# A planned order for attention and two expert layers: new priorities, and instruction packets in the planner's model of the DMA rings

## The chip, the cores and the metric

The kernel runs on one core of a Trainium2 chip. Its time is the device time in microseconds of one execution; where one number stands for a kernel it is the median of its timed runs. Five engines work beside each other and meet only at semaphores: TensorE (PE; its weight loads are shown apart as PEld), VectorE (DVE), ScalarE (ACT), GpSimd (POOL) and SyncE (SP), which issues the transfers here. A transfer is spread over 16 DMA engines.

## What is computed

Three stages follow one another. The first is a local attention beside an attention on a sequence that is reduced by four; the second a feed-forward layer with a rational activation; the third a feed-forward layer with h·tanh(softplus(h)).

```python
# q, k, v: [2, 8, 576, 64] float32
q_d, k_d, v_d = (mean of 4 neighbours along the sequence)            # 144 rows
out_up    = repeat(softmax(q_d k_d^T / 8) v_d, 4)
out_local = softmax(q k^T / 8 where |i - j| < 4, else -1e9) v
x = (out_up + out_local), as 1152 tokens x 512
h = x @ w_in1                                                        # 512 x 2048
P = a0 + a1 h + a2 h^2 + a3 h^3;  Q = 1 + |b0| |h| + |b1| h^2
x = (P / (Q + 1e-6)) @ w_out1                                        # 2048 x 512
h = x @ w_in2
out = (h * tanh(softplus(h))) @ w_out2
```

The weights arrive as 64-bit floats (read as int64 words) and are converted on the chip.

## The kernel before

**Attention.** There are 18 units: one batch, one pair of heads and four windows of 64 query rows each, two of them mixed (the last window of all four head pairs of a batch). A unit is a chain: SyncE loads q (L648) and four pieces of v windows (L665); TensorE flips q (L552, 128x128) and, after a copy by ScalarE or VectorE, makes the scores (L712 to L728); VectorE takes the maxima (L743) and subtracts them (L752), ScalarE takes exponentials (L759, L767), VectorE and GpSimd normalise (L772 to L786); TensorE transposes the result (L797, L802) and multiplies it with v (L827, L837); the sum goes to x as a high and a low part (L857 and behind). Each of the eight pairs of heads needs its keys loaded and flipped once (L560, L564, L552 with 96 columns) and its v reduced (L614). There are two buffers for v windows and three for q, so a load of windows waits for the value products of the unit two before it.

**Weights.** They come in grains of 1 MB (L994 for the first matrix of a layer, L999 for the second), into two raw buffers. ScalarE converts in two steps (L1011, L1018), VectorE joins them (L1025; for most grains of the last layer also L1031), and a high and a low part are split off (L1037, L1042).

**Products.** Each product of float32 is made of three passes (high by high, low by high, high by low). L1155 are those of the second stage's first matrix, L1288 and L1290 those of the second matrices, L1469 and L1525 those of the third stage's first matrix. They follow the attention in chunks of tokens, so the products of the first chunk (256 tokens) start while later chunks are still in attention. VectorE and ScalarE evaluate the activation between the two matrices (for the first group by a division on VectorE, L1184 to L1255).

**What sets the order.** Nothing is ordered by hand. While the program is built, `Plan.run` simulates the engines with a cost per task, and each engine that is free takes the ready task of lowest priority number. Instructions are emitted in the order in which this simulation starts them, and on the chip each engine keeps that order and waits where it must. The priorities come from constants and two tables: `PROL` and `PSTEP` space the attention units of the first chunk, `LEAD` says how far the later ones run ahead of the products that need them, `UOFF` shifts each of the 18 units; `LOFF`, `KOFF`, `VOFF` and `VROFF` shift the loads of q, k, v windows and v; `LLEAD` and `CLEAD` put the loads and the conversion of weights ahead of their first use, `OLAG` shifts the second matrices, `GOFF` the first twelve grains. Where TensorE has nothing to do in the simulation and the recent share of it is under `FILL`, a dummy product of zeros (L533) is put in. The model of transfers has one queue: a transfer starts after the one before it has moved, at most eight are under way (`QUEUED`).

The functions that the diff touches:

Of the kernel before, what the change touches and what calls it, by code (L numbers as in the profile page):

```python
# [25 lines left out]

SECOND = 1.8
COLD, FILL_ALL = 3.4, 20
WINDOW, FILL, FILL_END = 3.4, 0.9, 450.0
SHOW = (2.4, 30.0)  # L30
LEAD, CLEAD, LLEAD, OLAG = 38, 14, 40, 18
PROL, PSTEP, VOFF, VROFF, LOFF, KOFF = -45, 2.5, 2, -1, 7, 9
GROUPS = ([6, 6, 4], [4, 4, 4, 4])
KCUT, MIX = 4, (1, 4)
MKP = -45
# [3 lines left out]
NRAW, NWT, NRING, NRING2 = 2, 2, 3, (2, 1)  # L39
LAT = {"pe": 0.2, "act": 0.16, "dve": 0.15, "pool": 0.15, "sp": 1.1}  # L40
QUEUED = 8
UOFF = [-3.0, 0.0, 0.0, 3.0, 4.5, 3.0, 3.0, -1.5, 6.0, 0.0, 0.0, -4.5, -4.5, 4.5, 6.0, 4.5, -1.5, -1.5]
GOFF = [0.0, 0.0, 0.0, 0.0, -4.0, -4.0, -10.0, -6.0, 2.0, -4.0, 10.0, 12.0]
HP = 15


# [34 lines left out]
class Plan:  # L81
# [33 lines left out]
    def run(self, names):  # L115
# [3 lines left out]
        landed, moved = [0.0] * QUEUED, 0.0  # L119
# [76 lines left out]
        while True:  # L196
            for e in names:
# [3 lines left out]
                while ready[e]:  # L201
# [18 lines left out]
                    end = until[e] = begin + t.engs[e] * (2 if e == "pe" and now < COLD else 1)  # L220
                    there = end + LAT[e]
                    if t.dma:
                        end = begin
                        for issue, move in t.dma:
                            end = max(end, landed[-QUEUED]) + issue
                            moved = max(moved, end + 0.3) + move
                            landed.append(moved + LAT["sp"])
                        until[e], there = end, landed[-1]
                    n += 1
# [13 lines left out]
                if e == "pe" and until[e] <= now:  # L243
                    got = fill()
                    if got:
                        b, dur = got
                        end = until[e] = now + dur * (2 if now < COLD else 1)
# [27 lines left out]
def kernel(  # L275
# [26 lines left out]
    add = plan.add  # L302
# [184 lines left out]
    t_id = add({"pool": 1.1}, lambda: make_identity(nc, ident), -1000)  # L487
    t_m = add({"dve": 0.1}, lambda: nc.vector.memset(band, 0.0), -1900)
    t_cd = add({"dve": 0.6}, zeros, -1000)
    add({"dve": 0.4}, lambda: None, -880)  # L490
    t_bn = add({"pool": 0.5}, bands, -900, after=[t_m])
    def mask_set(lo, hi, ws):
        for w in ws:
            masks(*w)
# [2 lines left out]
    t_mk = [  # L497
        add({"dve": cost}, lambda x=x: mask_set(*x), pr, after=[t_bn])
        for cost, pr, x in (
            (0.4, -890, (0, 4, ((0, 0, 1), (0, 1, 1), (0, 2, 1), (0, 3, 1)))), (0.25, MKP, (3, 7, ((1, 4, 4),))),  # L500
            (0.25, MKP, (7, 11, ((2, 8, 4),))),
        )
    ]
    t_bias = add({"pool": 0.1}, biases, -20)
# [129 lines left out]
    def unit(u, slots, start):  # L634
        bb, kind, wins, prio, nw, n = u.bb, u.kind, u.wins, u.prio, NW, 32 * NW
        pairs = sorted({p for p, _ in wins})
        mixed = len(pairs) > 1
# [68 lines left out]
        def pe_b():  # L706
# [24 lines left out]
                        )  # L731

        tb = add(
            {"pe": 1.6 if mixed else 0.86}, pe_b, prio,
            after=tq + [kv_done[p] for p in pairs] + [t_i16, t_mk[kind]],
            take=[sc, tm, s, pd],
            use=[qT] + mix, chain="pb",
# [157 lines left out]
    first = [(0, 256), (256, 256), (512, 256), (768, 384)]  # L895
# [689 lines left out]
```

## Time and profile before

| | |
|---|---|
| timed runs | 477.99, 479.17, 482.95 us; median 479.17 |
| profiled execution | 481.31 us, its span 479.5 us |
| mean granted TensorE clock | 0.993 |
| busy, share of the span | PE 98%, PEld 89%, DVE 79%, ACT 70%, POOL 12% |
| instructions | 9855; 4081 matmuls |
| transfers | 47.17 MB, 97 GB/s over the span |

The span runs from the first to the last instruction of the profiled execution. Busy time is shown for each engine; matmuls are pipelined, so that their rows overlap. A row of a timeline has its start in the span, its duration, engine, source line, operation, what it writes and reads, and in square brackets the idle time of that engine before it, with the engine that ended it. In a stretch, the column PEclk is the TensorE clock that was granted, as a share of full speed: 1.00 and 0.50 are its two levels, 2.4 and 1.2 GHz.

### The profile page before, as it was taken

How to read it: one execution, taken by the hardware profiler on the slowest of the kernel's cores; microseconds unless marked ns; L12 is line 12 of the kernel's file. 1: busy time of each engine (PE TensorE's matmuls, PEld its weight loads, DVE VectorE, ACT ScalarE, POOL GpSimd, SP SyncE). 2: the span in 40 equal slices, each digit the busy share in tenths (PEclk: the TensorE clock that was granted, in tenths of full speed). 3: DMA queues.
4: the chain of work that ended last, by engine and by line, in shares of the span. 5: the costliest groups of instructions: out<-in, count | busy, mean ns of one | idle time of the engine just before them, and what ended most of it. 6: DMA issues, size and time to landing. Idle time of an engine off the chain costs nothing.

```text
span 479.5 us, 9855 instructions
## 1 busy us (share of the span) xinstructions
PE 467.6 (98%) x4081; PEld 428.5 (89%) x4081; DVE 376.8 (79%) x566; ACT 337.6 (70%) x529; POOL 58.7 (12%) x80
## 2 busy tenths in 40 slices
PE   8999898999999999999999999999999999999996
PEld 4667797889999999999999998898989898989885
DVE  6688789899899978997999989988596669524342
ACT  5778698885988799998878797578667446422320
POOL 2654345653000000000000000000000000000000
PEclk9999799999999999999999999999999999999999
DMA  8967976611422402333022022134314220000103
GB/s 180 234 172 176 263 184 182 153 42 36 168 89 90 143 34 87 106 130 117 0 89 89 1 89 87 45 115 143 137 21 156 87 89 0 1 0 2 66 1 131
DMA packets 45757, 47.17 MB, mean 98 GB/s; under 512 B 30352, under 2 KB 31120, under 8 KB 45712
## 3 DMA queue, kind: packets, MB, share of 16 engines
q1 hardware_dynamic: 45712, 46.54, 33.4%
q8 instruction: 32, 0.52, 0.5%
q14 instruction: 13, 0.11, 0.1%
HBM read 44.17 MB, written 2.36 MB: 97 GB/s over the span
## 4 chain that ended last, share of the span: by engine, by line
PE 74%; DVE 12%; DMA 8%; ACT 3%; issue 1%; SPq 1%; ACTq 0%
PE psum L1290 19%; PE psum L1155 18%; PE psum L1288 15%; PE psum L1469 11%; PE psum L1525 5%; DMA att<-in_q_dram 3%; DMA raw<-in_moe_w_in_dram 3%; PE psum L837 1%; DMA att<-in_v_dram 1%; PE psum L827 1%; DVE wt L1025 1%; PE psum L552 1%; DVE xl L1311 1%; DVE wrk L1329 1%; PE psum L728 1%
## 5 line engine op out<-in xcount | busy, mean ns | idle before, releaser
L1155 PE MATMUL psum<-xh,wi 128*128 128x384 f32 (+1 forms) x336 | 84.7, 323 | 0.2 <-DVE wrk L1184 0.2
L1288 PE MATMUL psum<-gg,wo 128*128 128x384 f32 (+1 forms) x480 | 76.2, 313 | 0.0
L1288 PEld LDWEIGHTS psum<-gg,wo 128*128 128x128 f32 x480 | 72.8, 189 | 0.5 <-issue 0.2
L1155 PEld LDWEIGHTS psum<-xh,wi 128*128 128x128 f32 x336 | 60.2, 193 | 1.5 <-issue 0.9
L1155 PE MATMUL psum<-xl,wi 128*128 128x384 f32 (+1 forms) x168 | 53.1, 316 | 0.0
L1290 PE MATMUL psum<-wo,gg 128*128 128x512 f32 x216 | 51.7, 391 | 0.0
L1290 PE MATMUL psum<-wo,late_g 128*128 128x512 f32 x216 | 51.3, 391 | 0.0
L1290 PEld LDWEIGHTS psum<-wo,late_g 128*128 128x128 f32 x216 | 40.4, 188 | 8.0
L1290 PEld LDWEIGHTS psum<-wo,gg 128*128 128x128 f32 x216 | 40.4, 188 | 8.0
L1025 DVE SCALAR_TENSOR_TENSOR wt<-wt,raw 128x1024 int32<-128x1024 int32 x32 | 40.4, 1266 | 7.5 <-ACT wt L1011 6.5
L1011 ACT ACTIVATE wt<-raw 128x1024 f32<-128x1024 f32 x32 | 36.4, 1137 | 8.7 <-DVE wo L1042 4.8
L1018 ACT ACTIVATE raw<-raw 128x1024 int32<-128x1024 uint16 x32 | 36.8, 1149 | 4.7 <-DMA raw<-in_moe_w_out_dram 3.4
L1525 PE MATMUL psum<-xh,wi 128*128 128x384 f32 x128 | 34.5, 335 | 0.0
L1155 PEld LDWEIGHTS psum<-xl,wi 128*128 128x128 f32 x168 | 32.5, 193 | 0.0
L1401 DVE TENSOR_TENSOR part<-psum,part 128x512 f32<-128x512 f32 x27 | 17.8, 687 | 13.6 <-PE psum L1290 13.6
L1155 PE MATMUL psum<-xh,late_r 128*128 128x384 f32 x96 | 25.5, 334 | 0.0
L1175 ACT ACTIVATE wrk<-psum 128x768 f32<-128x768 f32 (+1 forms) x27 | 19.9, 735 | 6.6 <-PE psum L1155 6.0
L1037 ACT ACTIVATE wo<-wt 128x1024 fp32r<-128x1024 f32 x11 | 11.7, 1061 | 17.7 <-DVE wt L1031 7.7
L1042 DVE TENSOR_TENSOR wo<-wt,wo 128x1024 fp32r<-128x1024 f32 x14 | 17.1, 1218 | 8.7 <-ACT wo L1037 8.7
L1525 PEld LDWEIGHTS psum<-xh,wi 128*128 128x128 f32 x128 | 23.3, 188 | 0.2
L1099 ACT ACT_TABLE_LOAD x17 | 21.8, 1283 | 0.3
L1525 PE MATMUL psum<-xl,wi 128*128 128x384 f32 x64 | 21.4, 335 | 0.0
(164 smaller groups left out, 1038.5 us busy)
## 6 DMA issues: line engine op xcount, KB each, us to landing
raw<-in_moe_w_in_dram SPq DMA_DIRECT2D x16, 1024.0 KB, 5.4
raw<-in_moe_w_out_dram SPq DMA_DIRECT2D x16, 1024.0 KB, 4.9
att<-in_v_dram SPq DMA_DIRECT2D x72, 48.0 KB, 4.0
out_dram<-part SPq DMA_DIRECT2D x9, 256.0 KB, 2.0
att<-in_q_dram SPq DMA_DIRECT2D x16, 128.0 KB, 3.9
att<-in_k_dram SPq DMA_DIRECT2D x6, 288.0 KB, 3.8
att<-in_v_dram SPq DMA_DIRECT2D x6, 288.0 KB
wrk<-in_k_dram SPq DMA_DIRECT2D x2, 288.0 KB, 6.2
```

Of the source, the lines that this page charges most:

```text
L1011: nc.scalar.activation(out=t.v, in_=words(r)[:, :, 1].bitcast(F32), func=AF.Prelu if fold else AF.Identity, scale=2.0 ** -112, **({"alpha" ...
L1018: nc.scalar.activation(out=words(r)[:, :, 0], in_=r.v.bitcast(U16).rearrange("p (n four) -> p n four", four=4)[:, :, 1], func=AF.Copy, sca ...
L1025: nc.vector.scalar_tensor_tensor(out=ti, in0=ti, scalar=3, in1=words(r)[:, :, 0], op0=ALU.logical_shift_left, op1=ALU.bitwise_or)
L1042: ENG[e].tensor_tensor(out=w.v[:, 1], in0=s.v, in1=w.v[:, 0].bitcast(F32), op=ALU.subtract)
L1099: nc.scalar.preload_act_table_set(name)
L1155: nc.tensor.matmul(st.h.v[:, i, :T], w.v[:, ww, ks], xx[:, kk, c0:c0 + T], start=(nn == 0 and (st.big or i == 0)), stop=(nn == 3 * KD - 1 ...
L1175: nc.scalar.activation(out=vw(st.a), in_=H(), func=AF.Square)
L1288: nc.tensor.matmul(A(d)[:, :T], w.v[:, ww, lo + d * 128:lo + (d + 1) * 128], vw(gg)[:, i, :], start=start, stop=stop)
L1290: nc.tensor.matmul(A(d), vw(gg)[:, i, sl], w.v[:, ww, lo:lo + DM], start=start, stop=stop)
L1401: nc.vector.tensor_tensor(out=pv, in0=acc.v[:, j], in1=pv, op=ALU.add)
L1469: nc.tensor.matmul(dst.v[:, :TW], wv.v[:, ww, at:at + 128], x(h, kk), start=bool(take) and nn == 0, stop=nn == 5, skip_group_check=not take,)
L1525: nc.tensor.matmul(h.v[:, i, :TW], w.v[:, ww, at:at + 128], xx[:, kk, c0:c0 + TW], start=nn == 0, stop=nn == 3 * KD - 1)
```

## The change

It alters the costs and priorities that the planner works with, and one rule in its model. Line numbers of the changed program are higher by one from the model of transfers on.

```diff
-WINDOW, FILL, FILL_END = 3.4, 0.9, 450.0
-SHOW = (2.4, 30.0)
-LEAD, CLEAD, LLEAD, OLAG = 38, 14, 40, 18
-PROL, PSTEP, VOFF, VROFF, LOFF, KOFF = -45, 2.5, 2, -1, 7, 9
+WINDOW, FILL, FILL_END = 3.4, 0.7, 450.0
+LEAD, CLEAD, LLEAD, OLAG = 38, 20, 30, 26
+PROL, PSTEP, VOFF, VROFF, LOFF, KOFF = -45, 3.0, 2, 2, 5, 9
...
-UOFF = [-3.0, 0.0, 0.0, 3.0, 4.5, 3.0, 3.0, -1.5, 6.0, 0.0, 0.0, -4.5, -4.5, 4.5, 6.0, 4.5, -1.5, -1.5]
-GOFF = [0.0, 0.0, 0.0, 0.0, -4.0, -4.0, -10.0, -6.0, 2.0, -4.0, 10.0, 12.0]
+FETCH = (0.8, 7.0)
+SHOW = (2.4, 30.0)
+UOFF = [1.5, 0.0, 1.5, 9.0, 13.5, 13.5, 6.0, 18.0, 13.5, 9.0, 3.0, -6.0, -7.5, -3.0, 9.0, 12.0, -7.5, -7.5]
+GOFF = [0.0, 2.0, 8.0, 4.0, 0.0, -4.0, -4.0, -22.0, 18.0, 0.0, -6.0, 24.0]
...
                         for issue, move in t.dma:
                             end = max(end, landed[-QUEUED]) + issue
-                            moved = max(moved, end + 0.3) + move
+                            first = max(moved, end + 0.3)
+                            moved = first + move + FETCH[0] * (int((first + move) / FETCH[1]) - int(first / FETCH[1]))
                             landed.append(moved + LAT["sp"])
...
-    add({"dve": 0.4}, lambda: None, -880)
-    t_bn = add({"pool": 0.5}, bands, -900, after=[t_m])
+    t_bn = add({"pool": 1.0}, bands, -900, after=[t_m])
...
-            (0.4, -890, (0, 4, ((0, 0, 1), (0, 1, 1), (0, 2, 1), (0, 3, 1)))), (0.25, MKP, (3, 7, ((1, 4, 4),))),
-            (0.25, MKP, (7, 11, ((2, 8, 4),))),
+            (0.8, -890, (0, 4, ((0, 0, 1), (0, 1, 1), (0, 2, 1), (0, 3, 1)))), (0.5, MKP, (3, 7, ((1, 4, 4),))),
+            (0.5, MKP, (7, 11, ((2, 8, 4),))),
...
-            {"pe": 1.6 if mixed else 0.86}, pe_b, prio,
+            {"pe": 1.52 if mixed else 0.78}, pe_b, prio,
```

`FETCH` adds 0.8 us to a modelled transfer each time it passes a multiple of 7 us: the time in which instruction packets take the rings. The costs of the mask's set-up rise, an empty task that stood in for some of it goes, and the scores' cost falls by 0.08. The rest is numbers.

In the built programs the work is the same, but for two things: 66 dummies instead of 61, and one copy of 128x768 sums that ScalarE made (L1368) is now made by VectorE (L512). All else is moved. Three places show how.

On SyncE, around the first load of weights: L665 are pieces of v windows, L648 loads of q, raw_74 is the first raw buffer of weights; in brackets stand the semaphores waited for. Before:

```order
L665 DMA att<-in_v_dram 48x4x64 [waits DMAHW2_49]
L648 DMA att<-in_q_dram 128x4x64 [waits DMAHW3_49,PE_49]
L994 DMA raw_74<-in_moe_w_in_dram 128x4x256 [waits DMAHW4_49]
L648 DMA att<-in_q_dram 128x4x64 [waits DMAHW5_49,PE_49]
L665 DMA att<-in_v_dram 48x4x64 [waits DMAHW6_49,PE_49]
L665 DMA att<-in_v_dram 48x4x64 [waits DMAHW7_49,PE_49]
L665 DMA att<-in_v_dram 48x4x64 [waits DMAHW0_49,PE_49]
```

In the changed program, one line higher each:

```order
L666 DMA att<-in_v_dram 48x4x64 [waits DMAHW4_49,PE_49]
L666 DMA att<-in_v_dram 48x4x64 [waits DMAHW5_49,PE_49]
L666 DMA att<-in_v_dram 48x4x64 [waits DMAHW6_49,PE_49]
L666 DMA att<-in_v_dram 48x4x64 [waits DMAHW7_49]
L649 DMA att<-in_q_dram 128x4x64 [waits DMAHW0_49]
L995 DMA raw_74<-in_moe_w_in_dram 128x4x256 [waits DMAHW1_49]
```

The four pieces that wait for TensorE stood behind the first weights and stand ahead of them now.

On TensorE, from the tenth unit's scores (the first two rows) on: L827 and L837 are value products, L552 flips of k (96 columns) and q (128), L797 and L802 transposes of the softmax, L1288 products of the second matrix. Before, the tenth unit's transposes are the last two rows:

```order
L720 MATMUL psum<-att 32x48 x16
L728 MATMUL psum<-att 32x144 x4
L827 MATMUL psum<-att 64x64 x4
L837 MATMUL psum<-att 64x32 x16
L797 MATMUL psum<-ident,att 112x128 x2
L802 MATMUL psum<-ident,att 72x128 x2
L1288 MATMUL psum<-gg,wo_81 128x256 x12
L552 MATMUL psum<-ident,att 128x96 x6
L552 MATMUL psum<-ident,att 128x128 x2
L797 MATMUL psum<-ident,att 112x128 x2
L802 MATMUL psum<-ident,att 72x128 x2
```

In the changed program the tenth unit's scores are again the first two rows, its transposes the last two:

```order
L721 MATMUL psum<-att 32x48 x16
L729 MATMUL psum<-att 32x144 x4
L798 MATMUL psum<-ident,att 112x128 x2
L803 MATMUL psum<-ident,att 72x128 x2
L828 MATMUL psum<-att 64x64 x4
L838 MATMUL psum<-att 64x32 x16
...
L721 MATMUL psum<-att 32x48 x16
L729 MATMUL psum<-att 32x144 x4
L798 MATMUL psum<-ident,att 112x128 x2
L803 MATMUL psum<-ident,att 72x128 x2
```

Before, the unit ahead had its values and its transposes there, and twelve products and eight flips besides; now one set of transposes, one of values and the scores of the next unit are all that is between.

On VectorE, the same unit's softmax: L743, L744 are the maxima, L752 the subtraction, L772 to L776 the sums and their reciprocals; L1213 and L1218 belong to the activation, L857 to another unit's sum. Before:

```order
L743 TENSOR_REDUCE att<-psum 128x4
L744 TENSOR_REDUCE att<-psum 128x1
L1213 SCALAR_TENSOR_TENSOR wrk<-wrk 128x512
L857 TENSOR_TENSOR att<-psum,att 128x256
L752 TENSOR_TENSOR att<-psum,att 128x4x48
L1218 SCALAR_TENSOR_TENSOR wrk<-wrk,cf 128x512
L772 TENSOR_REDUCE att<-att 128x4
L773 TENSOR_SCALAR att<-att 128x5
L776 RECIPROCAL att<-att 128x5
```

In the changed program:

```order
L744 TENSOR_REDUCE att<-psum 128x4
L745 TENSOR_REDUCE att<-psum 128x1
L753 TENSOR_TENSOR att<-psum,att 128x4x48
L1026 SCALAR_TENSOR_TENSOR wt_76<-wt_76,raw_74 128x1024
L773 TENSOR_REDUCE att<-att 128x4
L774 TENSOR_SCALAR att<-att 128x5
L777 RECIPROCAL att<-att 128x5
L858 TENSOR_TENSOR att<-psum,att 128x256
```

Two steps of the activation and the other unit's sum no longer stand between the tenth unit's maxima and its reciprocals; a join of weights (L1026) does.

## Rows read from the trace of the kernel before

**Rows 1.** The page's first part: busy time, share of the span and instructions.

```profile
PE 467.6 (98%) x4081; PEld 428.5 (89%) x4081; DVE 376.8 (79%) x566; ACT 337.6 (70%) x529; POOL 58.7 (12%) x80
```

**Rows 2.** Stretches: from:to, length, busy (instructions) per engine, PEclk, DMA share, GB/s.

```profile
50.00:60.00 10.00, 8.50 (x114) 7.41 (x113) 7.09 (x15) 5.58 (x14) 4.03 (x5) 0.66 1.00 271
60.00:120.00 60.00, 57.42 (x1134) 51.41 (x1133) 55.45 (x115) 49.26 (x115) 29.80 (x34) 1.00 0.48 119
120.00:310.00 190.00, 189.14 (x1116) 187.34 (x1114) 174.42 (x196) 162.37 (x190) 0.75 (x1) 1.00 0.25 84
```

**Rows 3.** Timeline of SyncE's queue: start, time (us), engine, line, operation.

```profile
15.37 0.51 SPq L994 DMA_DIRECT2D raw<-in_moe_w_in_dram  x1
16.84 0.61 SPq L648 DMA_DIRECT2D att<-in_q_dram  x1
17.55 2.04 SPq L665 DMA_DIRECT2D att<-in_v_dram  x4
...
36.75 3.33 SPq L665 DMA_DIRECT2D att<-in_v_dram  x4
```

**Rows 4.** Timeline of TensorE, 13.6 to 16.5 us.

```profile
13.70 0.38 PE L797 MATMUL psum<-ident,att 128*112 128x128 f32 x2
...
14.13 0.57 PE L533 MATMUL psum<-blank 128*128 128x480 bf16 x2
14.63 0.26 PE L712 MATMUL psum<-mask,eye 64*32 64x192 bf16 x4
...
15.41 0.45 PE L827 MATMUL psum<-att 72*64 72x64 f32 x8
...
16.39 0.30 PE L552 MATMUL psum<-ident,wrk 96*128 96x96 f32 x1
```

**Rows 5.** Timeline of ScalarE: the first weight conversion's two steps.

```profile
22.91 1.14 ACT L1011 ACTIVATE wt<-raw 128x1024 f32<-128x1024 f32 x1
...
24.55 1.15 ACT L1018 ACTIVATE raw<-raw 128x1024 int32<-128x1024 uint16 x1
```

**Rows 6.** Timeline of TensorE; in brackets idle time before and what ended it.

```profile
30.77 0.46 PE L1155 MATMUL psum<-xh,wi 128*128 128x256 f32 x1
...
39.94 0.41 PE L552 MATMUL psum<-ident,att 128*128 128x128 f32 x2 [0.51 <-DMA att<-in_q_dram]
...
52.51 1.03 PE L837 MATMUL psum<-att 48*64 48x32 f32 x30 [1.50 <-DMA att<-in_v_dram]
...
76.57 0.69 PE L552 MATMUL psum<-ident,att 96*128 96x96 f32 x5 [1.13 <-ACT att L593]
77.99 0.40 PE L797 MATMUL psum<-ident,att 128*112 128x128 f32 x2 [0.72 <-POOL att L786]
```

**Rows 7.** The stretch behind the wait at 52.51, columns as before.

```profile
52.60:59.40 6.80, 6.80 (x95) 6.02 (x96) 4.18 (x9) 3.59 (x9) 1.62 (x3) 0.50 1.03 250
```

**Rows 8.** Landing times of one line's loads: L994 first, then L648.

```profile
DMA to landing us min/median/max: 5.2/5.4/7.9
...
DMA to landing us min/median/max: 2.1/3.9/6.6
```

**Rows 9.** Timeline of all engines, 71.7 to 78.1 us: TensorE and VectorE rows.

```profile
71.79 0.41 PE L728 MATMUL psum<-att 64*32 64x144 f32 x8
...
72.88 0.35 DVE L743 TENSOR_REDUCE att<-psum 128x4 f32<-128x192 f32 x1
...
73.36 0.74 DVE L1213 SCALAR_TENSOR_TENSOR wrk<-wrk 128x512 f32<-128x512 f32 x1
...
73.52 1.68 PE L1288 MATMUL psum<-gg,wo 128*128 128x256 f32 x12
...
74.62 0.73 DVE L1218 SCALAR_TENSOR_TENSOR wrk<-wrk,cf 128x512 f32<-128x512 f32 x1
```

**Rows 10.** Groups by form, VectorE: busy us, mean ns, idle before and releaser.

```profile
L1025 DVE SCALAR_TENSOR_TENSOR wt<-wt,raw 128x1024 int32<-128x1024 int32 x32 | 40.4, 1266 | 7.5 <-ACT wt L1011 6.5 <-ACT raw L1018 0.6 <-DMA att<-in_v_dram 0.4
```

**Rows 11.** DMA queues, 0 to 60 us: packets, MB, share of 16 engines.

```profile
q8 instruction: 8, 0.13, 1.0%
```

## The prediction

> **What bounds the kernel now.** I read the busy times first, then the stretches, then the waits inside the stretch that is not full. TensorE is busy for 467.6 of 479.5 us [rows 1]. The stretches [rows 2] show where the remaining time lies: from 120 to 310 us it misses 0.86 of 190 us, so there the products alone set the time and a new order of the same products can win nothing. From 50 to 60 it misses 1.5 and from 60 to 120 2.6 us. The early stretch holds the attention, whose loads, softmax and weight conversions decide when TensorE can go on. From 60 to 120 VectorE is as full as TensorE (55.45 of 60 us), so a faster TensorE there soon meets VectorE. Behind 310 us nothing differs but a few swaps of full work. So the change is worth what it does to TensorE before 120 us. All waits of TensorE there that matter are in [rows 6]: 0.51 us at 39.94 for a q load, 1.50 at 52.51 for a v load, 1.13 at 76.57 and 0.72 at 77.99. The wait for v has a second price: right behind it the granted clock stands at 0.50, the lower of its two levels, for 6.8 us [rows 7], which costs 6.8 / 2 = 3.4 us. So some 7 us are on the table: 1.5 + 3.4 + 1.85 + 0.5.
>
> **The base of the sum.** The profiled execution took 481.31 us, 1.81 more than its span. The median of the three timed runs is 479.17, that is 2.1 less; I make the sum against 481.31 and subtract 2.1 at the end.
>
> **First products.** Now SyncE issues the first weight load at 15.37, before the third set of v windows (17.55) [rows 3]. In the new order that set stands before the weights, and it waits for TensorE: there are two buffers for windows, so the third set needs the first unit's value products, which end at 16.39 [rows 4]. The part ahead of them in the order is nearly the same, so I keep 16.39. Behind it come the set (2.04 us of issue) and one q (0.61): the weights go out at 16.4 + 2.0 + 0.6 + 0.1 = 19.1, 3.7 later. What is queued behind this wait is every later load; who waits is ScalarE (conversion), then all products. But the queue is shorter then: the load lands 5.4 us after its issue at the median [rows 8], so at 24.5, against a conversion that starts at 22.91 now [rows 5]. That is 1.7 us late, no more. From there to the first product it takes 30.77 - 22.91 = 7.9 us now [rows 5, 6]; 0.5 us of these are exponentials between the two conversion steps (24.55 - 22.91 - 1.14), which the new order has ahead of both. First product at 24.6 + 7.4 = 32.0, 1.2 late; one more value product (16.39 - 15.41 = 0.98 [rows 4]) is then already done. Net +0.3. Bounds: a landing of 5.2 to 7.9 us [rows 8] and a chain up to 1 us shorter give -0.9 to +2.8. The five more dummies (0.25 us each [rows 4]) all stand ahead of the first product, in time that this chain sets anyway: nothing. Were the chain early by as much, they would cost up to 1.25; that lies inside the bounds.
>
> **The tenth q.** q loads are issued closer to their use. The tenth stands behind the seventh set of windows, which waits for the fifth unit's value products. From there SyncE needs 2.04 for the set, and the load lands 2.1 to 6.6 us (median 3.9) after issue [rows 3, 8]: 4.1 to 8.6, at the median 5.9. TensorE has seven steps until it wants this q: two q flips at 0.41 [rows 6], two sets of transposes at 0.43, scores 0.78, values 0.98 [rows 4], and six products, 0.84 by the row of twelve such in 1.68 [rows 9]. Together 4.3 us. The queue is short there, as it is at the weights, so I take a landing of 3, between the lowest and the median, and a wait of 5.04 - 4.28 = 0.8, against the 0.51 that goes: +0.3. Bounds -0.5 to +3.8.
>
> **The v wait, and the tenth unit.** The wait at 52.51 comes behind two weight loads issued together. The new order puts window sets between the weights, so I take the 1.50 off. Also the 1.13 and 0.72 belong to the tenth unit: between its scores (end 72.20) and its transposes (77.99) [rows 6, 9] TensorE has two sets of output products, a flip of k and other work, and still waits. In the new order nothing but one set of transposes, one of values and one of scores stands there: 0.43 + 0.98 + 0.78 = 2.2 us [rows 4]. What must pass: 77.99 - 72.20 = 5.8 now, of which VectorE started 0.7 late (72.88) and spent 2.0 on foreign operations (73.36 to 74.62 + 0.73) [rows 9], so 3.1 are the unit's own; in the new order one join of weights (1.27 [rows 10]) stands inside: 4.4. Wait 4.4 - 2.2 = 2.2 us, bounds 0.9 (join hidden whole beside the exponential) to 3.6 (as long as now). Term: -1.50 - 1.85 + 2.2 = -1.15.
>
> **The clock.** The new wait of 2.2 us is longer than the one of 1.50 that the lower clock followed, and comes after 3.5 us of attention without products; the pieces of 1.13 and 0.72, with products between, were not followed by it (60 to 120 us ran at 1.00 [rows 2]). So I expect one half-clock stretch of the same size in the new place: 0. Bounds -3.4 (none) to +3.4 (two).
>
> **The rest.** From 60 to 120 VectorE has 4.5 us of idle time [rows 2]; units 14 and 15 now have some 2 us of TensorE work between q flip and scores, and their q copy can stand behind other VectorE work: +0.3, bounds 0 to +1.5. One copy of sums moves from ScalarE to VectorE after 140 us: about one operation of [rows 10]'s size, hidden in 190 - 174.4 = 15.6 us of VectorE idle time [rows 2]; without that cover it would cost 1.
>
> **Sum.** 0.3 + 0.3 - 1.15 + 0 + 0.3 = -0.25. 481.3 - 0.25 - 2.1 = **479.0 us**.
>
> **What the change counts.** Instruction packets are 8 in the first 60 us, 1.0% of 16 queues, that is 0.01 x 16 x 60 / 8 = 1.2 us each on one queue [rows 11]. A load lands when its last queue is done, so such a packet can put off a load by about 1.2 us at most, eight times. That is enough to shift single waits, not to remove a stage. The Trainium skill ("Runtime: NRT & Kernel Launch", Instruction fetch mechanics) calls the cost of these refills mostly hidden; by it the packets need no count at all and the new order would stand where the old did, 479.2. No row here shows an engine waiting for its instructions, but this row does show that they take queue time.
>
> **Rivals.** (1) No half-clock stretch: the tenth unit's wait is near its lower bound, or is split by other waits as at 76 to 78 us. For it: those two pieces did no harm. Against: 1.5 us in one piece did. 479.0 - 3.4 = 475.6. Chance 0.27. (2) Slower: the tenth q lands as late as 6.6 us, as q did where weights were in the queue. Then TensorE stands 8.6 - 4.3 = 4.3 us, 3.5 more than in my sum; it decides from the point where this wait passes 1.5 us, since then the lower clock follows here as well (+3.4). At a landing of 4.5 us (a wait of 2.3): 2.3 - 0.8 + 3.4 = +4.9, 483.9, at 6.6: 485.9. For it: a set of windows took up to 3.33 us of SyncE in the old order, against the 2.04 of my sum [rows 3]. Against: the weights of that time have landed by then. Chance 0.17. (3) The counted packets decide nothing and losses only change place: 479.2. Chance 0.14. My forecast has 0.42.
>
> **Range and chances.** 473.8 to 484.8: it takes in most of the forecast's bounds, rival 1 with 1.8 to spare and rival 2's nearer half. One per cent, about what can be told from no change here, is 4.8 us. Faster than 474.4 needs rival 1 and a first product before 30.8: 0.17. Slower than 484.0 is the most of rival 2 and a tail of the forecast: 0.14. Within: 0.69.
>
> **What would show it.** First weights issued near 19 and first product near 32 us. A wait of about 2 us at the tenth unit's transposes between 50 and 56 us, named after GpSimd, and a granted clock of 0.50 behind it; no wait for v of 1.5 us. From 120 to the end TensorE full. I am wrong if a full clock stands behind a wait of 2 us (rival 1), if TensorE waits longest for a q before 45 us (rival 2), or if VectorE's idle time from 60 to 120 shrinks to nothing and TensorE waits for it there.

## The result and the profile after

The changed kernel takes 485.87 us (median of six runs, 484.92 to 487.49) against 481.33 for the kernel before in six runs beside it: a ratio of 1.0127, with a 95% interval of 1.0088 to 1.0166. The forecast was 479.0, in a range of 473.8 to 484.8. Beside the experiments the kernel before has 93 fast runs, with a median of 479.0 us. The profiled execution of the changed kernel took 485.38 us, its span 483.6, which is 4.1 more than the span before.

The page's busy line and the stretches of the changed kernel, which answer to [rows 1, 2], and the one behind its clock's fall, which answers to [rows 7] (from:to, length, busy time of PE, PEld, DVE, ACT and POOL with instructions, PEclk, DMA share, GB/s):

```profile
PE 468.7 (97%) x4086; PEld 428.4 (89%) x4086; DVE 379.2 (78%) x567; ACT 338.7 (70%) x528; POOL 54.5 (11%) x80
...
50.00:60.00 10.00, 7.63 (x155) 6.28 (x158) 9.29 (x18) 8.56 (x22) 4.29 (x6) 1.00 1.07 239
60.00:120.00 60.00, 58.58 (x1067) 53.19 (x1055) 54.07 (x110) 48.18 (x110) 27.91 (x34) 0.94 0.54 145
120.00:310.00 190.00, 190.00 (x1179) 188.00 (x1178) 175.97 (x198) 161.82 (x192) 2.21 (x2) 1.00 0.24 81
...
53.00:62.00 9.00, 5.59 (x146) 3.70 (x145) 8.93 (x19) 8.39 (x18) 3.13 (x5) 1.00 1.02 214
62.00:68.80 6.80, 6.50 (x81) 6.03 (x81) 5.44 (x10) 4.86 (x12) 3.44 (x6) 0.50 0.52 114
```

TensorE is full from 120 us on, as before. It is busy 1.1 us more, about what the five more dummies take, and idle 3.0 us more; that makes the 4.1. The loss is all ahead of 120 us. From 50 to 60 us TensorE is busy for 7.6 of 10 us, and there is one stretch of 6.8 us at half clock, as in the trace before, 9 us later; so between these two traces the clock makes no difference.

The waits of TensorE in the changed kernel (engine, output, line, what it waited for: us in total, times, the longest), which answer to [rows 6]:

```profile
PE psum L534 <- DVE band L490: 1.2, 1, 1.2
PE psum L553 <- DMA att<-in_q_dram: 1.2, 3, 0.6
PE psum L798 <- ACT att L813: 1.1, 1, 1.1
PE psum L828 <- POOL att L625: 1.0, 1, 1.0
PE psum L1470 <- DVE wrk L1492: 1.0, 1, 1.0
PE psum L798 <- POOL att L782: 0.9, 1, 0.9
PE psum L798 <- ACT att L594: 0.8, 1, 0.8
PE psum L729 <- issue: 0.8, 1, 0.8
PE psum L553 <- ACT att L683: 0.7, 1, 0.7
PE psum L828 <- DVE att L858: 0.5, 1, 0.5
PE psum L838 <- issue: 0.5, 1, 0.5
PE psum L803 <- POOL att L787: 0.4, 1, 0.4
PE psum L713 <- ACT att L760: 0.3, 1, 0.3
```

Up to 63 us the waits behind the first dummy are some 8.3 us (up to 120 us, 5.8 in the trace of the kernel before and 4.9 in its second trace), and behind 63 us there is none but the 1.0 us at L1470, which the kernel before has too (0.9 at L1469). Of the waits of [rows 6] the one for v is gone; a copy of k (0.84 us) and the tenth transposes (0.90 and 0.44) are waited for earlier, and others have come, eight in all between 43 and 63 us. "issue" is a wait that no semaphore explains; it has a part below.

The start, SyncE's queue, then ScalarE and TensorE, which answer to [rows 3, 5, 6]:

```profile
15.84 3.24 SPq L666 DMA_DIRECT2D att<-in_v_dram  x4
19.13 0.61 SPq L649 DMA_DIRECT2D att<-in_q_dram  x1
19.78 0.64 SPq L995 DMA_DIRECT2D raw<-in_moe_w_in_dram  x1
```

```profile
26.46 1.13 ACT L1012 ACTIVATE wt<-raw 128x1024 f32<-128x1024 f32 x1
```

```profile
32.26 0.45 PE L828 MATMUL psum<-att 72*64 72x64 f32 x8 [1.02 <-POOL att L625]
...
34.39 0.39 PE L1156 MATMUL psum<-xh,wi 128*128 128x256 f32 x1
```

The set of windows (L666) stands ahead of the weights (L995), which go out at 19.78 (forecast 19.1). The conversion starts at 26.46 (24.6), the first product at 34.39 (32.0): values that wait 1.02 us for the reduction of a v load stand ahead of it.

To see where time is lost or won, I added up TensorE's work without dummies, each operation at the time that it takes where TensorE is full, and noted when each kernel had done the same amount of this work (420 us in all). A second trace of the kernel before (b_again, below) and the experiment a_dummies stand beside it:

| work done, us | before | before, second trace | changed | a_dummies |
|---|---|---|---|---|
| 8 | 31.2 | 34.8 | 33.4 | 33.1 |
| 14 | 41.2 | 43.6 | 44.2 | 43.6 |
| 20 | 49.8 | 52.1 | 55.8 | 55.0 |
| 25 | 61.0 | 58.6 | 69.5 | 65.8 |
| 40 | 81.9 | 81.0 | 88.1 | 85.4 |
| 60 | 111.0 | 109.4 | 114.9 | 112.2 |
| 419 | 474.3 | 472.7 | 478.4 | 475.3 |

The changed kernel loses most between 43 and 70 us, gets 4.6 us back by 111 us, 2.6 of it where the kernel before has its own waits, and keeps 4.1.

### The profile page after: what moved, and what is told of

The parts are those of the page before. It is cut to its first block, busy times and chain, and to the rows that moved or that the text cites. A ratio compares the mean times of both kernels' runs of the same rounds, so it can differ in the third digit from the quotient of the medians.

```text
span 483.6 us, 9867 instructions
## 1 busy us (share of the span) xinstructions
PE 468.7 (97%) x4086; PEld 428.4 (89%) x4086; DVE 379.2 (78%) x567; ACT 338.7 (70%) x528; POOL 54.5 (11%) x80
## 4 chain that ended last, share of the span: by engine, by line
PE 72%; DVE 15%; ACT 5%; DMA 4%; issue 2%; SPq 1%; POOL 1%; POOLq 0%; DVEq 0%; ACTq 0%
PE psum L1291 18%; PE psum L1156 14%; PE psum L1289 13%; PE psum L1470 11%; PE psum L1526 5%; PE psum L838 2%; DMA att<-in_v_dram 2%; PE psum L828 2%; PE psum L553 1%; DMA raw<-in_moe_w_out_dram 1%; PE psum L534 1%; DVE wt L1026 1%; DVE wt L1070 1%; PE psum L729 1%; DVE wi L1043 1%
## 5 line engine op out<-in xcount | busy, mean ns | idle before, releaser
L1026 DVE SCALAR_TENSOR_TENSOR wt<-wt,raw 128x1024 int32<-128x1024 int32 x32 | 39.3, 1227 | 7.2 <-ACT raw L1019 4.6
L1402 DVE TENSOR_TENSOR part<-psum,part 128x512 f32<-128x512 f32 x27 | 17.8, 687 | 13.6 <-PE psum L1291 13.6
L1038 ACT ACTIVATE wo<-wt 128x1024 fp32r<-128x1024 f32 x12 | 12.7, 1060 | 15.3 <-PE psum L1291 5.4
L1536 ACT ACTIVATE wrk<-psum 128x768 f32<-128x768 f32 x7 | 5.7, 815 | 24.6 <-PE psum L1526 24.6
L1176 ACT ACTIVATE wrk<-psum 128x768 f32<-128x768 f32 (+1 forms) x27 | 19.8, 734 | 3.5 <-PE psum L1156 3.4
```

The source lines that it names most:

```text
L1026: nc.vector.scalar_tensor_tensor(out=ti, in0=ti, scalar=3, in1=words(r)[:, :, 0], op0=ALU.logical_shift_left, op1=ALU.bitwise_or)
L1176: nc.scalar.activation(out=vw(st.a), in_=H(), func=AF.Square)
L1402: nc.vector.tensor_tensor(out=pv, in0=acc.v[:, j], in1=pv, op=ALU.add)
```

## Experiments

The first four kernels change numbers of the planner. The others, but for b_again and the two fetch kernels, keep the planner's run: its tasks are collected in a list, and a few entries of this list are moved, left out or added before it is emitted, so that every engine keeps its order but for them. Line numbers of those kernels are some 20 higher. Times are medians; "clock" is the mean granted clock over a kernel's runs. Of the kernel before, 29 runs of 93 had a clock of 0.999 or more and took 478.4 us on average, 18 had 0.993 or less and took 482.1; the mean was 0.9960. The changed kernel's six runs lie between 0.986 and 0.993, mean 0.9893.

**Parts of the change.**

```diff
 # a_weights_old: the changed kernel with
-LEAD, CLEAD, LLEAD, OLAG = 38, 20, 30, 26      # and GOFF as before
+LEAD, CLEAD, LLEAD, OLAG = 38, 14, 40, 18
 # a_att_old: the changed kernel with
-PROL, PSTEP, VOFF, VROFF, LOFF, KOFF = -45, 3.0, 2, 2, 5, 9      # and UOFF as before
+PROL, PSTEP, VOFF, VROFF, LOFF, KOFF = -45, 2.5, 2, -1, 7, 9
 # b_model: both, and FILL 0.9; only the model and the costs are the change's
 # a_nofetch: the changed kernel with
-FETCH = (0.8, 7.0)
+FETCH = (0.0, 7.0)
```

a_weights_old. 

> The changed kernel with LEAD, CLEAD, LLEAD, OLAG and GOFF of before (loads, conversions and products of weights), everything else as changed. Theory A (the changed plan takes weights and their products too late: first product 34.4 against 30.8 us, second weight load 31.0 against 23.2, third 45.4 against 32.9): 1.5 to 4 us less than the changed kernel, first product before 32.5 us, time lost up to 60 us of TensorE work at most 1.5 us more than before. Rival B (the attention's own offsets bunch the units; weights only follow): within 1.5 us of the changed kernel, 1.0 to 1.5% slower than before. Rival C (the model's counting of packets decides): the same as B.

a_att_old. 

> The changed kernel with PSTEP, VROFF, LOFF and UOFF of before (priorities of the attention units and their loads), everything else as changed. Theory A (late weights): no better than the changed kernel, 484 to 489 us, first weight load still behind 18 us. Rival B (attention's offsets): 1.5 to 4 us less than the changed kernel. Rival C (the model decides): within 1.5 us of the changed kernel.

b_model. 

> All priorities of before (LEAD to OLAG, PSTEP, VROFF, LOFF, UOFF, GOFF, FILL) under the changed model: packets counted, new costs of the mask and the scores. Theory A and rival B (numbers of the priorities decide): within 1% of before, 478 to 485 us. Rival C (the counted packets move the order to a worse one by themselves): 485 us or more.

a_nofetch. 

> The changed kernel with the counting of packets off (FETCH of 0.0), all its priorities and costs kept. If the counting is what makes this order late: 482 us or less. If the priorities were found together with the counting and fit no other model: 486 us or more, slower than the changed kernel. If it does not matter: within 1.5 us of the changed kernel.

Measured: a_weights_old 493.9 us (1.026, interval 1.017 to 1.036), a_att_old 489.4 (1.021, 1.015 to 1.028), b_model 482.6 (1.007, 1.005 to 1.010), a_nofetch 487.8 (1.018, 1.015 to 1.021). No part of the numbers explains the loss alone: each half undone alone is slower than the changed kernel, and both undone (b_model) is faster, so the two groups of numbers depend on each other. That speaks against theory A and rival B as I put them. The counting is not what makes the order late either (rival C): without it the same numbers give no shorter time (487.8 against 485.9), and with it and the new costs the numbers of before cost 0.7%.

**The clock.**

```diff
+# dummies ahead of a step of TensorE, by step and number of the unit, from 0
+# pe_b: a unit's scores, pe_d: its transposes, pe_e: its values
+MORE = {("pe_e", 7): 6}                                                    # b_dummies
+MORE = {("pe_e", 5): 2, ("pe_d", 7): 4, ("pe_d", 8): 5, ("pe_b", 10): 1, ("pe_d", 9): 4}   # a_dummies
```

b_dummies. 

> The kernel before with six dummy products (128x480, about 0.2 us each) put ahead of the eighth unit's value products, which wait 1.50 us for v at 51 to 52.5 us; all else keeps its order. Theory (the wait of 1.50 us is what the half-clock stretch of 6.8 us follows): no stretch at 0.50, or a later one, 3.4 us less where none comes, the wait shrinks to about 0.3 us. Rival (the clock falls for another reason): stretch stays at 52 to 59 us, time within 0.5 us of before or up to 1.2 us longer.

a_dummies. 

> The changed kernel with 16 dummy products (about 0.2 us each) ahead of the steps that wait between 43 and 62 us (2 ahead of the sixth unit's values, 4, 5 and 4 ahead of the eighth to tenth units' transposes, 1 ahead of the eleventh's scores); all else keeps its order. Theory G (half of the loss is the clock: over its runs the changed kernel has a mean granted clock of 0.989, before 0.996, which is 3 us; and idle TensorE there is what brings it down): mean clock 0.994 or more, time 2 to 3 us less. Rival H (the clock falls whether or not TensorE is kept busy in these waits): mean clock 0.987 to 0.991, time the same or up to 1 us longer.

b_dummies: 479.9 us, ratio 1.000 (0.996 to 1.004), clock 0.9966 over ten runs, in the trace no fall at 52 us but one of 3.4 us at 75.6. Over its runs the kernel before does not lose its clock by the wait of 1.50 us; the theory falls. The fall at 75.6 us comes right behind the waits of 1.11 and 0.72 us at the tenth unit's transposes. a_dummies: 483.1 us (482.0 to 484.5), 2.8 less than the changed kernel, though it runs 16 products more; its seven runs have a clock of 0.995 to 0.999. Timed beside it, a_v_first (below) stands for the changed kernel, with 485.8 us at a clock of 0.985 to 0.986. Theory G holds: in the changed kernel the clock falls because TensorE stands still so often between 43 and 62 us. The same two stretches in a_dummies:

```profile
53.00:63.00 10.00, 9.53 (x206) 5.75 (x208) 9.77 (x21) 9.91 (x23) 3.54 (x6) 1.00 1.07 200
62.00:68.80 6.80, 6.80 (x108) 6.58 (x105) 6.46 (x13) 6.71 (x15) 5.51 (x6) 1.00 0.54 97
```

From 53 to 63 us TensorE is busy for 9.53 us instead of 6.29 (the same stretch of the changed kernel stands with a_novec below), and the clock stays at 1.00 behind it.

**The start.**

```diff
+# entry of the list: (task, the entry that it goes in front of)
+MOVES = {153: ('vload', 129)}                                              # a_v_first
+MOVES = {153: ('vload', 129), 139: ('load', 113), 186: ('scale', 163), 191: ('low', 171), 201: ('join', 186),
+         216: ('hi', 200), 222: ('lo', 214), 230, 234, 239: (three products, 220)}   # a_first
+DROP = (208, 209, 212, 213, 217)                                           # dummies: a_first, a_start
+MOVES = {216: ('hi', 210), 222: ('lo', 219)}                               # a_start, a_start_d
+DROP = {..., 153: 'vload', 191: 'low', 201: 'join'}                        # a_start, a_start_d
```

a_v_first. 

> The changed kernel with the fourth v load (its line L615 at 21.9 us, landed near 30.1) issued right behind the third set of windows, ahead of one q and of the first weights; all else in its order. Theory D (the first products are late because the values ahead of them on TensorE wait 1.02 us for this v): the wait of 1.02 us at 32.3 goes, first product at 33.0 to 33.9 instead of 34.4, time 0.5 to 1.0 us less. Rival E (the weights' chain ends at 33.3 us and sets the first product anyway): first product stays at 33.9 to 35.0, the weights issued 0.6 us later, time the same within 0.5 us.

a_first. 

> The changed kernel with the start of before: first weight load ahead of the third set of windows, its conversion some 3.5 us earlier on ScalarE and VectorE, the fourth v load early, the first nine products ahead of the fourth unit's values, and the five dummies there left out; all else in its order. Theory D (late first products are most of the loss, and it is carried to the end): first product at 30 to 32 us, 2 to 3 us less than the changed kernel, 483 or under. Rival F (the stretch from 43 to 62 us, where units stand back to back, sets the end, and takes the gain up as longer waits): first product as early, but the gain under 1 us.

a_start. 

> The changed kernel with an early start by leaving work out: the fourth v load (the reduction takes what is in the buffer), two of the first weight conversion's steps (second ScalarE step and join) and five dummies at 30 us are left out, the conversion's last two steps stand one step earlier. Theory D (what the start loses is carried to the end, since TensorE has no waits behind 63 us): first product at 32.0 to 33.0 us instead of 34.4, and 1.3 to 2.5 us less than the changed kernel at the end at equal clock. Rival F (the full stretch from 53 to 63 us sets the end): the gain is gone by 63 us, as longer waits of TensorE there, and the time within 0.7 us of the changed kernel.

a_start_d. 

> a_start (early start by leaving work out: fourth v load, two steps of the first conversion, five dummies at 30 us) together with the 16 dummies of a_dummies between 43 and 62 us. Theory D with G (the start's loss is carried to the end, and in a_start the clock hid it): mean clock 0.995 or more, and 1.2 to 2.2 us less than a_dummies, that is 481 to 482. Rival F (the full stretch from 53 to 63 us takes the gain up): within 0.7 us of a_dummies, 482.4 to 483.8.

a_v_first: 485.8 us, the same. The wait for the reduction is gone, q loads are waited for instead (1.24 and 1.44 us in its trace), and the first product comes at 34.86, as rival E has it. a_first: 488.4, slower, at a clock of 0.982: with 1 MB of weights ahead of them the q loads come late, one of them by 3.06 us, and the first product comes at 35.59 instead of 30 to 32, so that it tests neither theory. In these two traces the start is bound by transfers as much as by order, and moving one load ahead makes the next one late. a_start, which leaves the work out, has its first product at 33.73, behind a wait for exponentials that takes most of the place:

```profile
32.96 0.26 PE L734 MATMUL psum<-mask,eye 64*32 64x192 bf16 x4 [0.98 <-ACT att L781]
...
33.73 0.39 PE L1177 MATMUL psum<-xh,wi 128*128 128x256 f32 x1
```

It ends at 485.0 us, but at a clock of 0.984. With the dummies that hold the clock (a_start_d, 0.997) it takes 482.5 against 483.1 of a_dummies. These 0.6 us lie in rival F's range, but they are no more than the kernel before differs by in the runs beside each of the two (478.4 and 479.5), and the traces of both kernels have their first product at the same time and work 10 at 35.8, a_dummies first:

```profile
34.09 0.39 PE L1176 MATMUL psum<-xh,wi 128*128 128x256 f32 x1
```

```profile
34.06 0.39 PE L1188 MATMUL psum<-xh,wi 128*128 128x256 f32 x1
```

So in this trace the first product was not brought forward as it was meant to be, and a_start_d cannot decide between D and F. Nor can a_start: it is 0.8 us faster than the changed kernel, at a clock that is lower by 0.005, and by the estimate for the clock in the next section that would be 2.8 us at an equal clock, on theory D's side. The second trace of the kernel before speaks against D: there the first product comes at 34.38 us, as late as in the changed kernel, and work 8 is reached at 34.8, yet it ends 1.6 us earlier than the first trace. How much of a late start is carried to the end stays open.

**The stretch from 53 to 63 us.**

```diff
+MOVES = {362: ('low', 371), 368: ('join', 375)}                            # a_conv
+DROP = {362: 'low', 368: 'join'}                                           # a_noconv
+DROP = {336: 'n_2', 345: 'n_3', 358: 'd_3', 361: 'd_2', 362: 'low', 368: 'join'}   # a_novec
```

a_conv. 

> The changed kernel with two steps of the third weight conversion moved behind the tenth unit's softmax: the second ScalarE step (L1019, 57.6 us) behind the tenth unit's exponentials, the join on VectorE (L1026, 58.8 us) behind its reciprocals; all else in its order. Theory I (the waits of TensorE at 57 to 62 us are softmax time with conversion work standing in its chain, and TensorE never waits behind 63 us, so what is won here is kept): the waits at 59.7 and 61.4 us (0.30, 0.90) shrink by 1 us or more together, the same steps come 1.0 to 2.4 us earlier, time 1 to 2 us less than the changed kernel. Rival J (the products behind 65 us need these weights, which now come later): TensorE waits for VectorE's wi at 63 to 67 us instead, time the same within 0.5 us.

a_noconv. 

> The changed kernel without two steps of the third weight conversion: the second ScalarE step (1.18 us at 57.6) and the join (1.23 us at 58.8) are left out, nothing is moved. Theory M (from 53 to 63 us VectorE and ScalarE are the bound, and TensorE's waits there are time that it is behind them): the waits at 57 to 62.5 us (1.06, 0.30, 0.90, 0.44) shrink by 1.2 to 2.4 us together, and the end comes 1.2 to 2.4 us earlier at equal clock, more where the clock then stays up. Rival F2 (other links of the softmax chain fill the same time): waits within 0.5 us of now, time the same.

a_novec. 

> The changed kernel without six steps between 52 and 60 us, nothing moved: four activation steps on VectorE (L1219, L1224, L1195 and L1190, about 0.7 us each), the third conversion's second ScalarE step (L1019, 1.18) and its join (L1026, 1.23). Theory M (VectorE and ScalarE are full from 53 to 63 us, and TensorE waits for them): the waits from 54 to 62.5 us (0.84, 1.06, 0.30, 0.90, 0.44: 3.54 together) shrink to 2.0 or less, the tenth unit's values come 1.5 us or more earlier, and the end 1.5 us or more at equal clock. Rival N (the softmax's own chain of steps, with nothing of its own unit beside it, makes the waits): waits of 3 us or more stay, the end within 0.7 us at equal clock.

a_conv: 487.5 us, no gain; the waits there stay (0.84, 1.02, 1.02, 0.54), and 13.7 us run at half clock in its trace, so that the time says little on theory I. a_noconv: 485.9, the same; the waits are 0.85, 1.02 and 1.03 instead of 3.54 together, 0.6 less, in a trace that also runs 13.7 us at half clock. a_novec: 484.1 (ratio 1.011, interval 1.008 to 1.014). From 53 to 63 us, the changed kernel first, then a_novec:

```profile
53.00:63.00 10.00, 6.29 (x150) 4.03 (x151) 9.77 (x20) 9.28 (x22) 3.42 (x6) 0.95 1.00 211
```

```profile
53.00:63.00 10.00, 6.57 (x169) 4.88 (x169) 6.67 (x17) 8.97 (x23) 3.42 (x7) 0.95 0.95 209
```

VectorE falls from 9.77 to 6.67 us, and TensorE gains 0.28. The waits are still 0.85, 1.12, 0.90 and 0.44, 3.3 together: rival N, and theory M falls. The 1.8 us by which it ends earlier are no gain of the edit for certain: the clock was 0.991 for 0.989, some 0.8 us by the estimate in the next section, and the kernel before took 0.9 us less in the runs beside it than over all. A full VectorE is not the cause; ScalarE stayed nearly as full (8.97 for 9.28 us). What the tenth unit waits for can be read in the trace of a_novec (TensorE's L750 are its scores, L819 transposes; VectorE's L765 and L774 maxima and subtraction; ScalarE's L834 copies of transposes, L781 and L789 exponentials; VectorE's L794 the sums):

```profile
55.58 0.45 PE L750 MATMUL psum<-att 64*32 64x144 f32 x8
...
56.09 0.36 DVE L765 TENSOR_REDUCE att<-psum 128x4 f32<-128x192 f32 x1
...
56.58 0.35 DVE L774 TENSOR_TENSOR att<-psum,att 128x192 f32<-128x192 f32 x1
...
57.14 0.19 PEld L819 LDWEIGHTS psum<-ident,att 128*112 128x112 f32 x2 [1.41 <-ACT att L834]
...
57.83 0.65 ACT L834 ACTIVATE att<-psum 112x256 f32<-112x256 f32 x2 [0.74 <-PE psum L824]
...
58.38 0.38 ACT L781 ACTIVATE att<-psum,att 128x144 f32<-128x144 f32 x1
...
58.73 0.36 ACT L789 ACTIVATE att<-att 128x192 f32<-128x192 f32 x1
...
59.13 0.35 DVE L794 TENSOR_REDUCE att<-att 128x4 f32<-128x192 f32 x1 [2.20 <-ACT att L789]
...
60.65 0.18 PEld L819 LDWEIGHTS psum<-ident,att 128*112 128x112 f32 x2 [1.20 <-POOL att L803]
```

Maxima and subtraction are done by 56.9 us, at once behind the scores. The exponentials start at 58.38: in ScalarE's order they stand behind a copy (L834, 57.83) that needs the ninth unit's transposes, and these waited 1.12 us for the copy before. VectorE waits 2.20 us for the exponentials, GpSimd behind it, and the tenth transposes come at 60.65. From the end of the scores to there it is 4.6 us, against 4.7 in the changed kernel. Two units that stand back to back wait for each other in turn, and TensorE has no products in between. This is a reading of the trace; no edit changed ScalarE's order.

**The kernel before, again.**

```diff
+MOVES = {310: ('vload', 298)}      # b_set_first
+MOVES = {302: ('vload', 311)}      # b_v_behind
 # b_again: no edit
```

b_set_first. 

> The kernel before with the set of windows that the wait of 1.50 us at 52.5 stands for issued ahead of a q and a v load (some 1.6 us earlier); all else in its order. If that queue is the cause of the wait: the wait is 0.3 us or none, and without more waits elsewhere 1 to 1.5 us less than before, and up to 2 us more where the clock stays up. If the loads put behind it are waited for instead: same time within 0.5 us.

b_v_behind. 

> The kernel before with the v load of 288 KB at 46.1 us issued behind the set of windows that follows it, so that this set goes out 0.4 us earlier and has 288 KB less ahead of it. If that load's bytes are what the wait of 1.50 us at 52.5 us comes from: the wait shrinks by 0.8 to 1.5 us, time 0.5 to 1.5 us less, and the clock 1.000 in more runs than the 17 of 46 so far. If the bytes ahead of both are: wait within 0.4 us of 1.50, time the same.

b_again. 

> The kernel before, unchanged, for a second trace. If the waits that the profile calls issue depend on how full the rings happen to be, this trace may show some at the grid of 256 instructions where the first shows none; the waits that the order sets (1.50 us for v near 52, 1.13 and 0.72 us near 76 to 78) stay within 0.3 us.

b_set_first is void: its set goes into the buffer that the sixth unit's values still read, so that they take the eighth unit's windows and wait for them (3.31 us at 47 us); 483.7 us says nothing on the question. b_v_behind makes the edit rightly: 480.8 us, ratio 1.000 (0.997 to 1.003). Its trace has no wait for v near 52 us, but neither has b_again, which changes nothing. The waits of b_again:

```profile
PE psum L837 <- issue: 1.9, 1, 1.9
PE psum L533 <- DVE band L488: 1.2, 1, 1.2
PE psum L552 <- ACT att L593: 1.1, 1, 1.1
PE psum L552 <- DMA att<-in_q_dram: 1.0, 1, 1.0
PE psum L1469 <- DVE wrk L1491: 0.9, 1, 0.9
PE psum L797 <- POOL att L786: 0.7, 1, 0.7
```

The 1.50 us for v is missing, and with it the half clock at 52 us; a wait of 1.9 us named issue stands at 18.7 us, and the clock is at half for 3.4 us there and again from 76.4 us, right behind the waits of 1.13 and 0.73. So it has as much half clock as the first trace, at other places. The same values that waited for v until 52.51 us in the first trace start here at 53.07, without a wait, because TensorE comes to them later:

```profile
52.69 0.45 PE L827 MATMUL psum<-att 72*64 72x64 f32 x8
53.07 0.67 PE L837 MATMUL psum<-att 48*64 48x32 f32 x32
```

Only the waits that the order sets (1.13 and 0.73 at the tenth unit, 0.9 at L1469) are the same in both traces.

**Instruction packets.**

```diff
+for i in range(LOADS):              # 1 in fetch_quiet, 12 in fetch_busy
+    nc.sync.dma_start(out=raw[i], in_=...)            # 1 MB
+for i in range(1536):
+    nc.tensor.matmul(psum[:32, i % 2, :32], blank[:64, :32], blank[:64, :32], start=True, stop=True)
```

fetch_quiet. 

> Not the reference's computation: 20 products of 480 columns, then 1536 of 32 columns (with their weight loads 3072 instructions of TensorE), one 1 MB load at the start and nothing else on the DMA queues; the output is filled with zeros. Theory K (TensorE's instructions come in packets of 16 KB, and the waits that the profile calls issue are TensorE's for the next packet): packets every 256 instructions of TensorE, and issue waits at the same places of that grid, each 1.5 us behind a packet's end. Rival L (issue waits have another cause): no waits on that grid.

fetch_busy. 

> As fetch_quiet, with twelve 1 MB loads issued at the start, so that the rings are full while TensorE runs its 3072 instructions. Theory K, with packets that share the rings with the loads: packets take longer (over 0.9 us each, as in the kernels here) and start later, and the waits are longer by 0.5 us or more each than in fetch_quiet. Rival: the same waits as in fetch_quiet, the rings do not matter.

TensorE in fetch_quiet, then in fetch_busy:

```profile
16.73 3.57 PE L45 MATMUL psum<-blank 64*32 64x32 bf16 x128 [0.71 <-issue]
20.45 3.57 PE L45 MATMUL psum<-blank 64*32 64x32 bf16 x128 [0.15 <-issue]
24.18 3.57 PE L45 MATMUL psum<-blank 64*32 64x32 bf16 x128 [0.16 <-issue]
```

```profile
21.35 3.57 PE L45 MATMUL psum<-blank 64*32 64x32 bf16 x128 [2.63 <-issue]
27.55 3.57 PE L45 MATMUL psum<-blank 64*32 64x32 bf16 x128 [2.62 <-issue]
33.74 3.57 PE L45 MATMUL psum<-blank 64*32 64x32 bf16 x128 [2.62 <-issue]
```

Each group is 128 products with their weight loads, 256 instructions, at half clock in both kernels. Nearly each group starts behind a wait named issue: 0.15 to 0.71 us where the rings are idle, 2.2 to 2.6 us while the loads fill them. The packet records of fetch_busy have 16 KB packets at 18.91, 25.17 and 31.36 us, each about 1.1 us long, and TensorE goes on 1.3 to 1.4 us behind the end of each. Theory K holds but for the packets' length: full rings cost by starting the packet later, not by making it longer (1.0 to 1.1 us, against 0.9 to 1.4 with idle rings).

## Why the prediction was wrong

The measured 485.87 us lie 6.9 above the forecast. Of these, 4.3 lie between the traced executions (485.38 against 481.06, the sum before its last step) and 2.6 in that last step.

**The clock** failed in the last step, the 2.1 us that I took off because the kernel before's median lies that far under its traced execution. The changed kernel's median lies 0.5 above its own. I forecast one stretch at half clock in the place of the other, net 0 with bounds of -3.4 and +3.4, from one execution of each kind of wait, and in the pair of traces it is so (6.8 us in each). Over runs it is a matter of how often: the mean clock of 0.9893 against 0.9960 is 0.0067 x 486 = 3.3 us, some 2.6 by an estimate from the kernel before's own 93 runs (a line through them gives 0.79 us of time for each us of clock lost), and a_dummies gave back 2.8. That is nearly half of the 6.6 us between the means (485.98 and 479.42); against the six runs beside it, whose clock is not on record, the loss is 4.5. What the fall at 62.0 us followed was not one long wait but seven of 0.3 to 1.1 us within 19 us.

**The base** failed with it. I counted 1.50 us of wait and its half clock as the order's, to be won back. The second trace of the same kernel has neither, and the edits aimed at that wait (b_dummies, b_v_behind) changed no time. A wait for a transfer in one execution was no property of the order. Nor was it one that the waits of 1.13 and 0.72 us do the clock no harm, on which the clock term and rival 1 leaned: in b_again and b_dummies a fall of 3.4 us follows right behind them.

**The waits ahead of the tenth unit** had no term but 0.8 us for one q load. The sum gave each step that I had looked at its price, and took the rest of the attention as it was. Together with the base this is the step that failed between the traces. Measured are 1.02 + 0.78 + 0.54 + 0.72 + 0.53 + 0.84 = 4.4 us between 32 and 55 us, two of them for instructions. Of the rival that goes slower, the late tenth q, nothing was seen; the q waits are 0.43, 0.56 and 0.17 us, all ahead of 27 us.

**The tenth unit** came out as worked out: 2.2 us of wait were forecast (bounds 0.9 to 3.6), named after GpSimd, and it is 0.30 + 0.90 + 0.44 behind 1.06 for the ninth, in a chain of 4.7 us (4.4), but at 59.7 to 62.3 us, not between 50 and 56. That the wait lies in pieces did not keep the clock up, which was the condition of rival 1. The reason that I gave, the join of weights in the chain, is not shown to matter: without it (a_novec) the chain is as long, so that the size came out in part by luck.

**First products:** +0.3 with a first product at 32.0 was forecast, and 34.4 measured, 2.2 us behind in work against the first trace. The weights went out 0.7 us late (19.8 for 19.1), the conversion started 6.7 us behind that for 5.5, and the chain from there took 7.9 us for 7.4, the 1.02 us for v among them. What that is worth at the end stays open: in b_again the first product is as late (34.38) and the end is not.

**The rest** held: TensorE full behind 120 us, VectorE with enough idle time, the moved copy without a price. What the counted packets are worth was judged rightly as no stage (a_nofetch, b_model), but I looked at one side only, what a packet does to a load. The two waits named issue in the changed kernel, 0.78 and 0.53 us, stand 512 instructions of TensorE apart, on the grid that fetch_quiet shows, 1.5 us behind the ends of the packets of 35.95 and 46.89 us; both loads and attention are dense there. The Trainium skill (Runtime: NRT & Kernel Launch, Instruction fetch mechanics) calls such a refill mostly hidden. The trace agrees behind 120 us, where no such wait is seen, and not between 31 and 50 us: 1.3 us.

What is shown, then: nearly half of the loss is the clock, and dummies in the waits bring it back. The other 3 to 4 us go with TensorE's waits, 8.3 us against 5.8 and 4.9 in the two traces of the kernel before, most of them between 43 and 63 us in units that follow each other without products. This part is read from traces, for no edit took these waits away. It is not the fullness of VectorE (a_novec) and not the counting (a_nofetch); the late start is neither shown to be part of it nor ruled out. That ScalarE's order of copies and exponentials is the link which would have to be cut is read from one trace and was not tried. None of the kernels that were tried is faster than the kernel before.

## What to carry to other kernels

A wait for a transfer in one profile may be that execution's alone: before it is priced as something to win, a second trace of the unchanged kernel tells it from the waits that the order sets. Where an order is made anew, walk every stretch in which one engine does only short dependent steps and ask what else it has to do there; the waits that hurt were not at the steps that the change named. And many short waits close together can cost the clock, though none of them is longer than 1.1 us.

## What the runs showed of the hardware

TensorE's instructions come in packets of 16 KB, 256 at a time, and beside the loads these come late (fetch_busy). TensorE stood still at most packets when products were as short as 28 ns: 0.15 to 0.7 us with idle rings and 2.2 to 2.6 us with full ones. In the attention kernels such waits come and go with the execution (none in one trace of the kernel before, 1.9 us in the other, up to 3.5 us in the experiments), and they stand at the same places of the grid of 256. And the same program ran at a mean granted clock between 0.986 and 1.000, some 4 us apart; 16 dummies of 0.2 us each, put where TensorE would have waited, saved 2.8 us. Standing still is not all that the clock falls behind: in fetch_quiet it fell to half at 11.8 us, in the middle of short products that had run without a wait since 7.2 us.
